# Where blocks of channel mixing stand in a unit of attention: behind its transposes, or between the second transposing step and the third score step

## The chip, the cores and the metric

The kernel runs on one core of a Trainium2 chip. The metric is the device time of one execution in microseconds. Five engines work side by side, each through its own instructions in program order: PE (TensorE, matmuls), ACT (ScalarE), DVE (VectorE), POOL (GpSimd) and SP (SyncE, which here only issues DMAs).

## What is computed

Attention with pooled queries, then a Fourier mixing over tokens and channels, then a normalised two-layer channel mixing. B = 4, H = 8, 1152 keys, 576 pooled queries, head size 64, model width 512, hidden width 2048:

```
q_pool = q.reshape(B, H, S // 2, 2, D).mean(axis=3)
attn   = softmax(q_pool @ k^T / sqrt(D))
x      = (attn @ v), heads side by side           # 4 x 576 x 512
u      = x + real(fft over tokens and channels of x)
un     = (u - mean(u)) / sqrt(var(u) + 1e-6)
out    = u + max(un @ w_ch1, 0) @ w_ch2
```

## The kernel before

**Units.** Attention goes by pairs of heads (16 pairs) and by tiles of 128 queries: a unit (pr, j) is query tile j of both heads of pair pr; j = 4 is the half tile of 64 queries, with both heads in one tile. So there are 80 units of five kinds. `attention` (L292 to 374) is a generator that walks over the units. While it handles unit i it also computes the scores of unit i + 1 (`nxt`).

**Steps of a unit.** A *score step* (`s_piece`, L183) computes 384 of the 1152 keys' scores for both heads into two PSUM banks (six matmuls, L191), and DVE reads each bank into the SBUF tile `sp` with a running minimum (L197). There are three per unit. A *transposing step* (`t_step`, L220) transposes eight 128-key chunks of one head (16 small matmuls, L225) into two banks, which ACT or DVE copies into `pt` (L228); there is one for each head, and a third, *one-chunk step* for the ninth chunk of both (4 matmuls, copied into `ptc`). Then the exponentials of the next unit are issued on ACT (`s_exp`, L209), which need all three score pieces. Last comes the *value product* (`av`, L234, 36 matmuls, L242), which reads `pt` and `ptc` and is copied out by ACT (L248). For j < 3 the order on PE is: score, transpose, score, transpose, score, one-chunk transpose, value product. Where the next unit is a j = 4 one, all three scores come first; in a j = 4 unit there is one large transposing step only.

**Banks.** Seven PSUM banks, tag "t", are handed out in rotation to score pieces, transposes, blocks and the matmuls of transform and norm (`bank`, L90). An eighth belongs to the value product.

**What runs beside attention.** When four pairs (one batch) are done, `mid` (L753) does the transform (`dft`, L391) and the normalisation (`norm`, L493) of that batch, as a list of small operations, mostly on DVE, with matmuls in between. Then `ffn` (L667) supplies the channel mixing in *blocks* of 12 matmuls (L663 to 665): one of the first product ends with a relu on ACT (L685) and a subtraction on DVE (L686), one of the second with an addition on DVE (L700). A converter splits weights into two parts on ACT, DVE and POOL (L587 to 625), and a block loads the weights of later ones through SP (L654).

**What sets the order.** All instructions are put in program order by hand: engines follow the order in which the Python code issues them. `spend(pe)` (L795) is called after each step with its planned PE time (530 for a score step, 60 for a transposed chunk, 3 x 700 or 3 x 380 for the value product); it adds `pe * RATES[nb]` to a credit, where RATES is 0.98, 0.85, 0.8, 0.8 for 1 to 4 batches begun (L59), and moves a planned clock on, by which due events and operations of `mid` are issued (`pulse`, L800). Where `attention` yields, `background` (L822) issues blocks as long as credit is above zero; a block advances the clock by `half` = 1360 and costs twice that in credit. Once `lag[0]` is 0, matmuls of `mid` wait for such a place too (L805 to 809).

**Before and after the first batch.** `lag[0]` is 1 at first: value products run one unit late, and no blocks exist. When the first batch's normalised values are `ready`, `lag[0]` becomes 0 (L373). From then on a unit yields twice: at L369, behind the one-chunk transposes and ahead of the value product, and at L374, at its end. L369 is what the change touches:

```
            if not lag[0] or len(held) > 1:
                if not lag[0] or ready:
                    yield 0
                while len(held) > (lag[0] if nxt else 0):
                    finish(*held.popleft())
```

Of the kernel before, what the change touches and what calls it, by code (L numbers as in the profile page):

```python
# [54 lines left out]
def fused_kernel(ctx: ExitStack, tc: tile.TileContext, k2, q2, v2, w1, w2, cst, out):  # L55
# [34 lines left out]
    def bank(name="f"):  # L90
        return ps_t.tile([P, 512], F32, tag="t", name=name)
# [16 lines left out]
    def load_pair(pr):  # L108
        b, h = divmod(pr, H // 2)
        kh, kl, qr, kr, vs = alloc_pair()  # L110
        ds = [nc.gpsimd.dma_start(kh, k2[b, h]), nc.sync.dma_start(qr, q2[b, h]),
              nc.sync.dma_start(kr, k2[b, h]), nc.sync.dma_start(vs, v2[b, h])]
        if pr == 1:
            for d in ds:
                later(d)
        raw[pr] = kh, kl, qr, kr, vs
# [11 lines left out]
    def load_first():  # L128

        kh, kl, qr, kr, vs = alloc_pair()  # L130
        qh, ql = alloc_q()
        qkv[0] = kh, kl, qh, ql, vs

        def q_load(a, b):
            nc.sync.dma_start(qr[:, :, a:b], q2[0, 0][:, :, a:b])

        def q_part(a, b):
            eng = nc.gpsimd if a else nc.vector
            eng.tensor_tensor(qr[:, 0, a:b], qr[:, 0, a:b], qr[:, 1, a:b], op=ALU.add)
            nc.scalar.copy(qh[:, a:b], qr[:, 0, a:b])  # L140
            eng.tensor_tensor(ql[:, a:b], qr[:, 0, a:b], qh[:, a:b].bitcast(F32), op=ALU.subtract)  # L141

        def k_load(a, b):
            nc.sync.dma_start(kr[:, a:b], k2[0, 0, :, a:b])

        def k_part(a, b):
            nc.scalar.copy(kh[:, a:b], kr[:, a:b])
            for c in (slice(a, a + 192), slice(a + 192, b)) if a else (slice(a, b),):
                (nc.gpsimd if a else nc.vector).tensor_tensor(kl[:, c], kr[:, c], kh[:, c].bitcast(F32), op=ALU.subtract)  # L149

        def v_load():
            nc.sync.dma_start(vs, v2[0, 0])

        return q_load, q_part, k_load, k_part, v_load

    def prep_pair(pr):
        kh, kl, qr, kr, vs = raw.pop(pr)
        qh, ql = alloc_q()
        HW = QW // 2
        halves = (slice(0, HW), slice(HW, QW))  # L160
        for c in halves:
            nc.gpsimd.tensor_tensor(qr[:, 0, c], qr[:, 0, c], qr[:, 1, c], op=ALU.add)
        for i in range(4):
            c = slice(i * HT, i * HT + HT)
            nc.gpsimd.tensor_tensor(kl[:, c], kr[:, c], kh[:, c].bitcast(F32), op=ALU.subtract)
        qkv[pr] = kh, kl, qh, ql, vs

        def q_high():
            nc.scalar.copy(qh, qr[:, 0, :])
            for c in halves:  # L170
                nc.gpsimd.tensor_tensor(ql[:, c], qr[:, 0, c], qh[:, c].bitcast(F32), op=ALU.subtract)
        after(2600, q_high)
# [7 lines left out]
    def unit_tiles(pr, j):  # L180
        return [(2 * pr, j), (2 * pr + 1, j)] if j < 4 else [(2 * pr, 4)]

    def s_piece(pr, j, pc):  # L183
        kh, kl, qh, ql, _ = qkv[pr]
        tiles = unit_tiles(pr, j)
        c = slice(pc * 384, pc * 384 + 384)
        rows = [slice(0, D), slice(D, P)] if j < 4 else [slice(0, P)]
        ps = [bank("s")[:, :384] for _ in rows]
        for i, (q, k) in enumerate(((qh, kh), (ql, kh), (qh, kl))):
            for p, r in zip(ps, rows):  # L190
                nc.tensor.matmul(p, lhsT=q[r, j * P:j * P + P], rhs=k[r, c], start=i == 0, stop=i == 2)  # L191
        for p, k in zip(ps, tiles):
            if pc == 0:
                sp[k] = spp.tile([P, S], F32, tag="sp", name="sp")
                bia[k] = smp.tile([P, 3], F32, tag="bia", name="bia", bufs=6)
            bt = bia[k]
            nc.vector.tensor_scalar(  # L197
                sp[k][:, c], p, -0.0625, bt[:, pc - 1:pc] if pc else None,
                op0=ALU.mult, op1=ALU.min, accum_out=bt[:, pc:pc + 1],
            )  # L200
        return 530

    def s_exp(n, j):
        pr = n // 2
        if pr not in den:
            den[pr] = smp.tile([P, 9], F32, tag="den", name="den", bufs=3)
        t = sp[n, j]
        col = 5 * (n % 2) + j
        last_exp[0] = nc.scalar.activation(t, t, AF.Exp, bias=bia.pop((n, j))[:, 2:3], scale=-1.0,  # L209
                                           accum_out=den[pr][:, col:col + 1]).ins  # L210

    lag = [1]
# [79 lines left out]
    def attention():  # L292
        idle = gp.tile([P, 512], F32, tag="g", name="zero")
        nc.vector.memset(idle, 0.0)
        ps = bank()
        for n in (512, 512, 192):
            nc.tensor.matmul(ps[:, :n], lhsT=idle[:, :P], rhs=idle[:, :n], start=True, stop=True)
        q_load, q_part, k_load, k_part, v_load = load_first()
        k_load(*K0[0])
        q_load(*Q0[0])  # L300
        for c in K0[1:]:
            k_load(*c)
        nc.sync.dma_start(ident, cst[4, :, :P])
        q_load(*Q0[1])
        v_load()
        q_load(*Q0[2])
        units = [(pr, j) for pr in range(NP) for j in range(5)]
        k_part(*K0[0])
        q_part(*Q0[0])
        k_part(*K0[1])  # L310
        k_part(*K0[2])
        for pc in range(3):
            s_piece(0, 0, pc)
        q_part(*Q0[1])
        s_exp(0, 0)
        s_exp(1, 0)
        nc.sync.dma_start(onesm, cst[4, :, P:2 * P])
        q_part(*Q0[2])
        yield 2000
        held = deque()  # L320
        for i, (pr, j) in enumerate(units):
            if pr == 1 and j == 0:
                for x, (t, r) in enumerate(((cc1, P), (cs1, P), (cc2, 97), (cs2, 97))):
                    n, m = t.shape[1:]
                    for r0, r1 in ((0, r // 32 * 32), (r // 32 * 32, r)):
                        if r0 < r1:
                            nc.sync.dma_start(t[r0:r1], cst[x, r0:r1, :n * m].rearrange("p (a b) -> p a b", a=n))
            if pr + 1 < NP:
                if j == 0:
                    load_pair(pr + 1)  # L330
                if j == 2:
                    prep_pair(pr + 1)
            nxt = units[i + 1] if i + 1 < len(units) else None

            tiles = unit_tiles(pr, j)
            where = {}
            early = lag[0] and i % 2
            scores = deque(range(3) if nxt else ())

            def score():  # L340
                if scores:
                    spend(s_piece(*nxt, scores.popleft()))

            if nxt and nxt[1] == 4:
                for _ in range(3):
                    score()
            for x, k in enumerate(tiles):
                score()
                pt = t_tile(512, early)
                spend(t_step(pt, [(k, c) for c in range(8)], "av" if j < 4 and (x or lag[0] and i % 2) else "aa"))  # L350
                for c in range(8):
                    for y in (x,) if j < 4 else (0, 1):
                        where[y, c] = pt, c * D
            score()
            pt = t_tile(P, early)
            spend(t_step(pt, [(k, 8) for k in tiles], "aa"))
            for y in range(2):
                where[y, 8] = pt, y * D if j < 4 else 0
            score()
            for k in unit_tiles(*nxt) if nxt else ():  # L360
                s_exp(*k)
            for k in tiles:
                sp.pop(k)
            held.append((pr, j, where))
            if j == 4:
                after(3000 if pr % 4 < 3 else 1500, den_recip(pr))
            if not lag[0] or len(held) > 1:
                if not lag[0] or ready:
                    yield 0  # L369
                while len(held) > (lag[0] if nxt else 0):  # L370
                    finish(*held.popleft())
                    if lag[0] and ready:
                        lag[0] = 0  # L373
            yield 0  # L374
# [390 lines left out]
    ready = []  # L765
# [4 lines left out]
    def after(wait, fn):  # L770

        heapq.heappush(events, (now + wait, next(tick), fn))
# [22 lines left out]
    def spend(pe):  # L795
        nonlocal credit
        credit = min(credit + pe * RATES[nb], 4000.0)
        pulse(pe * (1.25 if lag[0] else 1.1))
# [132 lines left out]
```

## Time and profile before

| | |
|---|---|
| median of 3 runs | 967.57 us (967.31 to 971.88) |
| the profiled execution's own time | 966.58 us |
| its span in the profile | 964.8 us |
| granted TensorE clock, mean | 0.973 |
| PE busy | 905.6 us, 94% |
| DVE busy | 565.2 us, 59% |
| ACT busy | 509.6 us, 53% |
| POOL busy | 233.9 us, 24% |

Busy time is the union of an engine's instructions. Matmuls are pipelined, so their rows overlap: the time of a step is read from the start of its first matmul to the start of the next step's. A number in brackets behind a row is the idle time of the engine ahead of it, with the instruction that ended the wait. Tile names: `s` score bank, `sp` scores and exponentials, `t` transposing bank, `pt`/`ptc` transposed tiles, `o` value product, `f` banks of blocks, transform and norm.

### The profile page before, as it was taken

The numbers are of one execution on the slowest core, as the hardware profiler recorded it, in microseconds if no ns is written. First come the engines' busy times: TensorE is split into PE (matmuls) and PEld (weight loads), VectorE is DVE, ScalarE is ACT, GpSimd is POOL, SyncE is SP. The second block draws the span as 40 slices with busy tenths as digits, with TensorE's granted clock in tenths as the row PEclk, the third lists the DMA queues.
The fourth block names the chain that finished last, engine by engine and source line by source line (L and its number), as shares of the span: only waits on it lengthen the run. The fifth ranks groups of instructions, "written<-read, shape, count | busy, mean of one in ns | idle before, by whom it ended". The sixth has DMA issues, their size and how long they took to land.

```text
span 964.8 us, 22607 instructions
## 1 busy us (share of the span) xinstructions
PE 905.6 (94%) x9030; PEld 768.2 (80%) x9030; DVE 565.2 (59%) x1501; ACT 509.6 (53%) x1068; POOL 233.9 (24%) x299
## 2 busy tenths in 40 slices
PE   7998888887999979899999999999999999999998
PEld 5877777675777767688788778788887788999998
DVE  6776879877465787964645757554446633222222
ACT  6786787596476756776645547755532121101110
POOL 4045443255346263723031103030000000000000
PEclk9998998987999989989999999999999999999999
DMA  6333664343676844656454315333255456643432
GB/s 221 111 126 128 201 222 167 104 164 112 226 267 203 309 152 170 205 187 241 146 166 155 114 35 167 126 110 100 67 167 190 137 187 204 219 131 120 122 109 66
DMA packets 54413, 153.27 MB, mean 159 GB/s; under 512 B 15187, under 2 KB 18019, under 8 KB 54309
## 3 DMA queue, kind: packets, MB, share of 16 engines
q1 hardware_dynamic: 49972, 142.20, 44.2%
q0 software_dynamic: 2160, 8.85, 2.9%
q8 instruction: 71, 1.16, 0.5%
q10 hardware_dynamic: 2176, 0.79, 0.3%
q14 instruction: 34, 0.27, 0.1%
HBM read 129.06 MB, written 22.75 MB: 157 GB/s over the span
## 4 chain that ended last, share of the span: by engine, by line
PE 67%; DVE 10%; ACT 8%; DMA 7%; issue 5%; SPq 1%; POOL 1%; DVEq 0%; ACTq 0%; POOLq 0%
PE f L663 14%; PE f L665 12%; PE f L664 12%; PE o L242 10%; PE s L191 8%; PE t L225 5%; ACT sp L209 3%; DVE sp L197 3%; PE f L475 3%; DMA r<-rd 3%; DMA rd<-rs 2%; ACT pt L228 1%; DVE xs L418 1%; PE f L466 1%; SPq L273 1%
## 5 line engine op out<-in xcount | busy, mean ns | idle before, releaser
L209 ACT ACTIVATE sp<-sp,bia 128x1152 f32<-128x1152 f32 x144 | 180.5, 1256 | 42.5 <-DVE sp L197 42.1
L197 DVE TENSOR_SCALAR_CACHE_REDUCE sp<-s,bia 128x384 f32<-128x384 f32 x288 | 165.9, 613 | 11.3 <-PE s L191 7.6
L225 PEld LDWEIGHTS t<-ident,sp 64*128 64x128 f32 x2592 | 113.3, 141 | 58.8 <-DVE sp L197 24.1
L225 PE MATMUL t<-ident,sp 64*128 64x64 f32 x2592 | 127.9, 229 | 34.1 <-DVE sp L197 16.3
L242 PE MATMUL o<-pt,vs 128*64 128x128 f32 (+1 forms) x2560 | 154.3, 273 | 5.0 <-ACT x L248 2.5
L242 PEld LDWEIGHTS o<-pt,vs 128*64 128x64 f32 x2560 | 134.3, 142 | 25.4 <-issue 14.6
L228 ACT COPY pt<-t 128x512 f32<-128x512 f32 x211 | 114.6, 588 | 68.5 <-PE t L225 67.8
L686 DVE SCALAR_TENSOR_TENSOR g<-f,g 128x512 fp32r<-128x512 f32 (+1 forms) x80 | 50.8, 638 | 164.2 <-ACT g L685 164.2
L685 ACT ACTIVATE g<-f 128x512 fp32r<-128x512 f32 (+1 forms) x80 | 44.1, 553 | 194.4 <-PE f L665 194.4
L663 PE MATMUL f<-g,w 128*128 128x512 f32 (+1 forms) x320 | 123.0, 384 | 2.1 <-DVE sp L197 1.0
L663 PE MATMUL f<-unh,w 128*128 128x512 f32 (+1 forms) x320 | 122.4, 383 | 0.7 <-DVE sp L197 0.2
L664 PE MATMUL f<-unh,w 128*128 128x512 f32 (+1 forms) x320 | 118.8, 371 | 0.0
L665 PE MATMUL f<-unl,w 128*128 128x512 f32 (+1 forms) x320 | 118.7, 371 | 0.0
L664 PE MATMUL f<-g,w 128*128 128x512 f32 (+1 forms) x320 | 118.7, 371 | 0.0
L665 PE MATMUL f<-g,w 128*128 128x512 f32 (+1 forms) x320 | 118.6, 371 | 0.0
L191 PE MATMUL s<-ksh,qh 64*128 64x384 f32 (+1 forms) x432 | 105.4, 427 | 6.7 <-ACT pt L228 3.0
L197 DVE TENSOR_SCALAR_CACHE_REDUCE sp<-s 128x384 f32<-128x384 f32 x144 | 74.9, 553 | 50.9 <-PE s L191 48.8
L191 PE MATMUL s<-ksh,ql 64*128 64x384 f32 (+1 forms) x432 | 85.8, 341 | 0.6 <-POOL ql L141 0.6
L191 PE MATMUL s<-ksl,qh 64*128 64x384 f32 (+1 forms) x432 | 85.6, 341 | 0.3 <-POOL ksl L149 0.3
L700 DVE TENSOR_TENSOR x<-f,x 128x512 f32<-128x512 f32 x48 | 33.1, 689 | 76.7 <-PE f L665 76.7
L611 POOL TENSOR_TENSOR wa<-wa,wk 128x256 int32<-128x256 int32 x64 | 48.8, 783 | 107.3 <-DVE wa L607 80.8
L663 PEld LDWEIGHTS f<-g,w 128*128 128x128 f32 x320 | 60.4, 189 | 14.1 <-DVE sp L197 3.6
(110 smaller groups left out, 1342.3 us busy)
## 6 DMA issues: line engine op xcount, KB each, us to landing
w<-w SPq DMA_DIRECT2D x128, 512.0 KB
wraw<-in_w SPq DMA_DIRECT2D x32, 512.0 KB
w<-wraw SPq DMA_DIRECT2D x32, 512.0 KB
qr<-in_q SPq DMA_DIRECT2D x15, 640.0 KB
vs<-in_v SPq DMA_DIRECT2D x16, 576.0 KB
ksh<-in_k POOLq DMA_DIRECT2D x15, 576.0 KB, 6.0
kr<-in_k SPq DMA_DIRECT2D x15, 576.0 KB
out<-x SPq DMA_DIRECT2D x12, 256.0 KB
```

The source lines that it names most:

```text
L191: nc.tensor.matmul(p, lhsT=q[r, j * P:j * P + P], rhs=k[r, c], start=i == 0, stop=i == 2)
L197: nc.vector.tensor_scalar(sp[k][:, c], p, -0.0625, bt[:, pc - 1:pc] if pc else None, op0=ALU.mult, op1=ALU.min, accum_out=bt[:, pc:pc + 1],)
L209: last_exp[0] = nc.scalar.activation(t, t, AF.Exp, bias=bia.pop((n, j))[:, 2:3], scale=-1.0, accum_out=den[pr][:, col:col + 1]).ins
L225: nc.tensor.transpose(p[:, i * D:i * D + D], sp[k][r, c * P:c * P + P], ident[r, r])
L228: (nc.vector.tensor_copy if eng == "v" else nc.scalar.copy)(pt[:, x, :o], ps[x][:, :o])
L242: nc.tensor.matmul(to.rearrange("p (x q) -> p x q", x=2) if j < 4 else to, lhsT=qkv[pr][4][:, y, c, :], rhs=rhs, start=c == 0, stop=c == N ...
L611: nc.gpsimd.tensor_tensor(ai[:, c], ai[:, c], k[:, c], op=ALU.add)
L663: nc.tensor.matmul(ps, lhsT=ah, rhs=bh, start=first, stop=False)
L664: nc.tensor.matmul(ps, lhsT=al, rhs=bh, start=False, stop=False)
L665: nc.tensor.matmul(ps, lhsT=ah, rhs=bl, start=False, stop=last)
L685: nc.scalar.activation(g[:, 0, :], ps, AF.Relu)
L686: after(1000, lambda: nc.vector.scalar_tensor_tensor(g[:, 1, :], ps, 0.0, g[:, 0, :].bitcast(F32), op0=ALU.max, op1=ALU.subtract))
```

## The change

In a unit with `lag[0]` at 0, the first of the two yields stands between the second transposing step and the third score step, no longer behind the one-chunk step; in a j = 4 unit, between its large transposing step and the second score. The yield at the old place is left for the unit in which `lag[0]` is still 1 and a batch is ready. The yield at the end of the unit stays.

```diff
@@ -351,6 +351,8 @@
                 for c in range(8):
                     for y in (x,) if j < 4 else (0, 1):
                         where[y, c] = pt, c * D
+            if not lag[0]:
+                yield 0
             score()
             pt = t_tile(P, early)
             spend(t_step(pt, [(k, 8) for k in tiles], "aa"))
@@ -365,7 +367,7 @@
             if j == 4:
                 after(3000 if pr % 4 < 3 else 1500, den_recip(pr))
             if not lag[0] or len(held) > 1:
-                if not lag[0] or ready:
+                if lag[0] and ready:
                     yield 0
                 while len(held) > (lag[0] if nxt else 0):
                     finish(*held.popleft())
```

## Rows read from the trace of the kernel before

**Rows 1.** The page, first part: engine, busy us (share of the span), instructions
```profile
PE 905.6 (94%) x9030; PEld 768.2 (80%) x9030; DVE 565.2 (59%) x1501; ACT 509.6 (53%) x1068; POOL 233.9 (24%) x299
```

**Rows 2.** Busy time by stretch: from:to, length, each engine's busy us, granted clock, DMA
```profile
235.00:720.00 485.00, 462.10 (x4983) 380.16 (x4980) 299.45 (x801) 294.90 (x617) 139.39 (x175) 0.98 0.48 163
330.00:420.00 90.00, 78.64 (x828) 63.93 (x828) 75.21 (x178) 61.48 (x123) 46.48 (x54) 0.92 0.55 191
530.00:620.00 90.00, 86.16 (x962) 70.18 (x958) 59.74 (x167) 55.60 (x118) 12.45 (x16) 0.98 0.32 104
720.00:965.00 245.00, 240.03 (x1253) 219.46 (x1251) 91.03 (x192) 40.09 (x78) 0.00 (x0) 1.00 0.47 151
```

**Rows 3.** Waits of PE, 235 to 720 us: us in total, times, longest
```profile
PE t L225 <- DVE sp L197: 10.8, 11, 2.6
...
PE o L242 <- DVE pt L228: 2.0, 4, 0.9
PE f L529 <- DVE sq L523: 1.8, 2, 0.9
PE f L663 <- DVE sp L197: 1.2, 6, 0.2
```

**Rows 4.** Timeline of PE, a quiet unit: start us, us, instruction
```profile
438.77 0.45 PE L191 MATMUL s<-ksh,qh 64*128 64x384 f32 x2
...
440.95 0.42 PE L191 MATMUL s<-ksh,qh 64*128 64x384 f32 x2
...
441.56 0.28 PE L225 MATMUL t<-ident,sp 64*128 64x64 f32 x4
441.90 0.50 PE L663 MATMUL f<-unh,w 128*128 128x512 f32 x1
...
444.84 1.97 PE L242 MATMUL o<-pt,vs 128*64 128x128 f32 x32
...
446.96 0.50 PE L663 MATMUL f<-unh,w 128*128 128x512 f32 x1
```

**Rows 5.** Timeline of PE, two units with waits, in the stretches from 330 and 530
```profile
344.73 0.65 PE L225 MATMUL t<-ident,sp 64*128 64x64 f32 x14 [2.50 <-DVE sp L197]
...
348.62 0.47 PE L225 MATMUL t<-ident,sp 64*128 64x64 f32 x3 [2.59 <-DVE sp L197]
349.02 0.79 PE L663 MATMUL f<-unh,w 128*128 128x512 f32 x1
...
354.00 1.21 PE L242 MATMUL o<-pt,vs 128*64 128x128 f32 x18
...
545.43 0.65 PE L225 MATMUL t<-ident,sp 64*128 64x64 f32 x14 [1.09 <-DVE sp L197]
...
547.30 0.33 PE L225 MATMUL t<-ident,sp 64*128 64x64 f32 x3 [0.54 <-DVE sp L197]
547.83 0.70 PE L663 MATMUL f<-g,w 128*128 128x512 f32 x1 [0.20 <-DVE sp L197]
...
552.38 0.88 PE L242 MATMUL o<-pt,vs 128*64 128x128 f32 x12
```

**Rows 6.** Timeline of PE, a unit with no block ahead of its value product
```profile
499.28 0.98 PE L242 MATMUL o<-pt,vs 128*64 128x128 f32 x14 [0.39 <-ACT ptc L228]
```

**Rows 7.** Waits of PE, 20 to 235 us, before any block exists
```profile
PE t L225 <- ACT sp L209: 10.0, 13, 1.6
```

**Rows 8.** Groups by line, 235 to 720 us: instruction, count, busy us, mean ns, idle before
```profile
L209 ACT ACTIVATE sp<-sp,bia 128x1152 f32<-128x1152 f32 x84 | 105.3, 1256 | 29.3 <-DVE sp L197 29.2
L197 DVE TENSOR_SCALAR_CACHE_REDUCE sp<-s,bia 128x384 f32<-128x384 f32 x168 | 96.8, 612 | 2.6 <-PE s L191 0.4
...
L686 DVE SCALAR_TENSOR_TENSOR g<-f,g 128x512 fp32r<-128x512 f32 x32 | 22.1, 691 | 87.6 <-ACT g L685 87.6
...
L248 ACT COPY x<-o 128x128 f32<-128x128 f32 (+1 forms) x50 | 12.4, 248 | 33.0 <-PE o L242 33.0
```

**Rows 9.** Timeline at 21 us: a score step starts, VectorE starts reading its first bank
```profile
21.66 0.44 PE L191 MATMUL s<-ksh,qh 64*128 64x384 f32 x2
...
22.59 0.56 DVE L197 TENSOR_SCALAR_CACHE_REDUCE sp<-s 128x384 f32<-128x384 f32 x1 [1.40 <-PE s L191]
```

## The prediction

> **What bounds the kernel now.** I read the page first: the PE row is busy for 94% of the span [rows 1], so nothing on another engine matters unless PE waits for it. Then the busy time by stretch. The change acts only while attention and channel mixing run together, from about 235 us (where `lag[0]` becomes 0) to about 720 us; there PE works 462.1 of 485.0 us, and after 720 it works 240.0 of 245.0 [rows 2]. So 22.9 us of idle PE is all that a better order can win directly. The same rows show where it lies: 11.4 us in the 90 us from 330 and 3.8 us in the 90 us from 530, the stretches in which the transform and norm of a batch fall among the units, and there the granted clock is 0.92 and 0.98 instead of 1.00, so some PE work ran at 1.2 and not 2.4 GHz. Third, the waits of PE in the stage [rows 3]. The largest is of transposes for VectorE's reading of score pieces: 10.8 us in 11 waits. A transpose does not use the piece that is being read; it waits for its bank, one of seven in rotation. In the timeline four of the 11 (5.2 us, up to 2.50) come before the second transposing step, which takes over a bank of the first score piece, and seven (5.6 us, up to 2.59) before the third, one-chunk step, which takes over a bank of the second piece; one of the first kind and two of the second are shown [rows 5]. A block then waits once more for the next bank: 1.2 us in 6 waits. Fourth, one quiet unit in time [rows 4]: scores and transposes from 438.77, the block from 441.90, the value product from 444.84, the next block from 446.96. A block takes 444.84 - 441.90 = 2.94 us, the value product 2.12 us, a score and a transposing step (440.95 - 438.77) / 2 = 1.09 us.
>
> **The change part by part.** No instruction is added or removed; blocks, and the matmuls of transform and norm that stop there too, move from behind the one-chunk transposes to between the second transposes and the third score. I call that place the first stop, and the end of the unit, which stays, the last stop. The code paces blocks by credit: a block is issued where credit is above zero, and costs 2 x 1360 = 2720. At RATES 0.85 a unit with j < 3 now earns (3 x 530 + 2 x 480 + 120) x 0.85 = 2270 before the first stop and 3 x 700 x 0.85 = 1785 before the last, so blocks stand there in about 0.83 and 0.66 of the units. Afterwards it earns (2 x 530 + 2 x 480) x 0.85 = 1717 and 2337: about 0.63 and 0.86. The count of blocks stays; about one block in five units goes over to the last stop. Fifty units lie in the stage (50 copies behind the value product [rows 8]), thirty of them with j < 3.
>
> Bank waits before the third transposes and before the block, 5.6 + 1.2 = 6.8 us: with a block between, 2.94 us pass in which VectorE reads the second piece, so these go where the first stop has a block. With a share of 0.65 that is **-4.4 us** (bounds 0 and -6.8). What is late next is the value product, which wants VectorE's copy of the second transposes, and then the exponential of the third piece. The waits before the second transposes, 5.2 us, stand ahead of the moved block and I leave them: **0**, between -2.6 and +2.6, since VectorE now gets 2.94 us in the middle of a unit and less at its end.
>
> Clock: the block behind the 2.59 us wait takes 354.00 - 349.02 = 4.98 us and the one behind the 1.09 and 0.54 us waits 552.38 - 547.83 = 4.55 [rows 5], against 2.94 in the quiet unit: 2.04 + 1.61 = 3.65 us lost. The second of the two waits goes and the first stays, so I take half, **-1.8 us** (0 to -3.65). The Trainium skill (TensorE: Matmul & The Clock Gate, section "HAM oscillation — how this bites in real kernels") reckons the loss as half of the time at the low level. By the granted clocks the two stretches hold 0.08 x 90 x 2 + 0.02 x 90 x 2 = 18 us of low level [rows 2], so by it an estimated 9.0 us are lost and half of that is -4.5, which would put the sum 2.7 us lower. I go by the rows, because part of that time had no matmul to slow: PE was idle.
>
> Units left without a block at the first stop: there the value product follows its transposes at once and waits for their copies. The row of such a unit shows 0.39 us [rows 6]; in all 2.0 us in 4 waits [rows 3] and this one, so 2.4 / 5 = 0.48 each. Their share among units with j < 3 goes from 0.17 to 0.37: 0.20 x 30 = 6 more units, **+2.9 us** (bounds 0, where the copies are early, and 6 x 0.9 = 5.4).
>
> Cover taken away: the third score's pieces, then both exponentials, must be done before the next unit's transposes. Now block, value product and often a second block lie between. Afterwards, without a block at the last stop, only the one-chunk step, the value product and one score do: 441.90 - 440.95 = 0.95, plus 2.12, plus 0.61 (441.56 - 440.95) = 3.68 us from the start of the third score, and 1.09 more to the second transposes, 4.77. The chain: VectorE starts reading 22.59 - 21.66 = 0.93 us after the score starts [rows 9], 0.61 for the piece, 1.26 for an exponential [rows 8]: 2.80, and 4.06 for the second. That fits by 0.7 to 0.9 us. The block's own subtraction on VectorE, 0.69 us [rows 8], now stands ahead of the pieces and leaves 0 to 0.2. So a wait appears where one more operation falls in. Units with a block first and none last: (1 - 0.86) x 30 = 4, at 0 to 0.77 us, the mean of the waits for exponentials in the stage without blocks (10.0 us in 13 [rows 7]); I take 0.25: **+1.0 us** (0 to 3.1).
>
> Queues: the weight loads that a block issues on SP go out in the same order, and the events that feed POOL are run by the same planned clock; no wait of PE in the stage names a DMA or POOL [rows 3], and the block-to-block distances stay near 5 us, so I cost this at nothing; should the cover go, the price is a late weight tile. The stage before 235 us keeps its order, as the old condition and the new one both stop there only when `ready`.
>
> Sum: -4.4 + 0 - 1.8 + 2.9 + 1.0 = **-2.3 us**. The profiled execution took 966.58 us (span 964.8 and 1.8 around it), 1.0 below the median of 967.57; I set the sum against the median: **965.3 us**. About 0.5%, 4.8 us, is what a measurement of this kernel can tell from no change, so this counts as the same.
>
> **The rivals.** *The exponential becomes the wait (slower).* If transform and norm use up the credit so that the last stop is empty in half of the 50 units and not in 0.14, the pieces of the third score have only 3.68 us of cover in 25 units. For it: in the stage without blocks, with just this cover, PE waited 13 times for 0.77 us in some 29 units [rows 7]. Against it: blocks move towards that stop. Price: 25 x 13/29 x 0.77 = 8.6 us instead of 1.0, giving 972.9. The sum turns positive from some ten such units, one in five. The Trainium skill (PSUM — Partial Sum Buffer, section "Engine vs sequencer instructions") has VectorE's queue as strictly first in, first out, which would let the block's subtraction hold the pieces back; the 2.50 us that transposes waited while VectorE worked off older operations agrees [rows 5].
>
> *The busy stretches come loose (faster).* All of the 6.8 us goes, both slowed blocks run at 2.4 GHz (-3.65), and half of the 5.2 us before the second transposes goes, since VectorE is no longer behind when the next unit starts: -6.8 - 3.65 - 2.6 + 2.9 + 1.0 = -9.2, giving 958.4. For it: the two 330 us rows alone hold 5.1 us of wait and 2.0 us of slow block in one unit. Against it: VectorE has 75.2 of 90 us of work there [rows 2], and it does not get less.
>
> *The waits only move.* VectorE sets the pace in those stretches, so what is saved before the block is waited for after it: -4.4 and -1.8 vanish, +3.9 stays, 971.5. That the change does nothing at all would need credit that is never above zero at the new place; 0.63 speaks against it.
>
> **How the numbers follow.** Forecast 0.48, the exponential 0.17, the busy stretches 0.27, waits that only move 0.08. Below 962.7 counts as faster: the busy stretches and 0.06 of the forecast's own spread, 0.33. Above 972.4 as slower: the exponential and 0.02 more, 0.19. The rest, 0.48, is the same. The range reaches just past the faster rival and to the slower one: 957.5 to 972.9.
>
> **What would show it.** Right: transposes wait for score pieces fewer than 8 times in the stage and none over 1 us stands before the one-chunk step; no block takes over 4 us behind such a wait; value products wait for copies some ten times at 0.4 to 0.5 us; waits of transposes for exponentials stay under 2 us. Wrong: several microseconds of waits for exponentials, or the clock rows of 330 to 420 no higher than 0.92, or PE's idle sum near 22.9 us with other names.

## The result and the profile after

The change made the kernel slower: 978.37 us in the median (972.85 to 982.35) against 968.55 for the kernel before, a ratio of 1.0112 with a 95% interval of 1.0089 to 1.0135. The forecast of 965.3 us was wrong in sign, and the time lies above its range.

The page of the changed kernel, engines' line and the group of the value product:

```profile
PE 908.0 (93%) x9030; PEld 769.4 (79%) x9030; DVE 564.3 (58%) x1501; ACT 508.3 (52%) x1068; POOL 230.7 (24%) x299
...
L242 PE MATMUL o<-pt,vs 128*64 128x128 f32 (+1 forms) x2560 | 160.8, 276 | 14.2 <-DVE pt L228 6.3
```

The same group on the page before:

```profile
L242 PE MATMUL o<-pt,vs 128*64 128x128 f32 (+1 forms) x2560 | 154.3, 273 | 5.0 <-ACT x L248 2.5
```

Work is the same and its counts are the same [rows 1]. The value product is what grew: before it was busy for 154.3 us with 5.0 us of idle time ahead of its matmuls, now 160.8 and 14.2. Busy time is a union, so at an equal count it grows where matmuls overlap less, and where they take longer at the lower clock (1.2 GHz). In the timeline each makes up about half of the growth: 20 value products instead of 10 stall inside their run of matmuls, and 7 instead of 5 run at the lower clock.

Busy time by stretch, columns as in [rows 2]:

```profile
235.00:720.00 485.00, 457.80 (x4926) 375.31 (x4923) 291.01 (x790) 291.02 (x612) 136.25 (x174) 0.98 0.47 159
330.00:420.00 90.00, 79.31 (x807) 64.22 (x808) 72.34 (x176) 59.39 (x121) 42.23 (x55) 0.91 0.53 186
530.00:620.00 90.00, 85.67 (x961) 70.53 (x957) 61.30 (x167) 53.19 (x115) 12.36 (x14) 1.00 0.34 109
720.00:965.00 245.00, 243.95 (x1263) 221.96 (x1262) 95.71 (x195) 42.12 (x82) 0.00 (x0) 1.00 0.50 156
```

PE idles 27.2 us in the stage, before 22.9 [rows 2]. The busy stretch from 330 us is no better: 10.7 us idle instead of 11.4, and a granted clock of 0.91 instead of 0.92. Waits of PE from 235 to 720 us, columns as in [rows 3]:

```profile
PE o L242 <- DVE pt L228: 6.3, 8, 1.8
PE o L242 <- ACT ptc L228: 3.7, 7, 1.1
PE t L225 <- DVE sp L197: 3.5, 6, 1.8
...
PE t L225 <- ACT pt L228: 2.5, 1, 2.5
PE o L242 <- ACT pt L228: 1.9, 5, 0.7
PE t L225 <- ACT sp L209: 1.3, 3, 0.8
```

The bank waits that the prediction went after did shrink, from 10.8 us to 3.5. In their place stand waits of the value product for its transposed copies: 6.3 + 3.7 + 1.9 = 11.9 us, where [rows 3, 6] have 2.0 and 0.4. In the timeline the block behind the last value product starts 6.6 us later than before (at 713.57 and not 706.94), and by then 57 blocks are done instead of 58; the missing one, 2.94 us, comes behind it. That makes up the 9.6 us by which the span grew (974.4 against 964.8).

A quiet unit without a block at the first stop, on PE and then on VectorE:

```profile
696.56 0.43 PE L242 MATMUL o<-pt,vs 128*64 128x128 f32 x2
697.39 1.82 PE L242 MATMUL o<-pt,vs 128*64 128x128 f32 x29 [0.39 <-DVE pt L228]
...
699.47 0.50 PE L665 MATMUL f<-g,w 128*128 128x512 f32 x1
```

```profile
695.47 0.62 DVE L197 TENSOR_SCALAR_CACHE_REDUCE sp<-s,bia 128x384 f32<-128x384 f32 x1
...
696.01 0.61 DVE L197 TENSOR_SCALAR_CACHE_REDUCE sp<-s,bia 128x384 f32<-128x384 f32 x1
...
696.55 0.69 DVE L228 COPY pt<-t 128x512 f32<-128x512 f32 x1
```

The value product starts, does two matmuls on the first head's copy and stops for the second's, which VectorE only begins at 696.55, behind both banks of the second score step. From its first matmul to the next block it takes 2.91 us, against 2.12 in a unit with a block ahead [rows 4]: 0.79 us, of which the row shows 0.39 as idle. Counted in program order, 24 of the 47 units from (6, 3) on, the first with lag 0 throughout, have no block at the first stop, before the change 13.

The second thing to see is one unit near 350 us, where a transform's operations and the third score meet. In the kernel before:

```profile
345.19 0.42 PE L191 MATMUL s<-ksh,qh 64*128 64x384 f32 x1
...
350.68 0.60 DVE L197 TENSOR_SCALAR_CACHE_REDUCE sp<-s,bia 128x384 f32<-128x384 f32 x1
...
351.33 1.26 ACT L209 ACTIVATE sp<-sp,bia 128x1152 f32<-128x1152 f32 x1 [1.87 <-DVE sp L197]
...
360.62 1.48 PE L225 MATMUL t<-ident,sp 64*128 64x64 f32 x36
```

The same unit in the changed kernel:

```profile
350.80 0.45 PE L191 MATMUL s<-ksh,qh 64*128 64x384 f32 x2
...
352.50 0.75 DVE L420 TENSOR_TENSOR xs<-x 128x576 f32<-128x576 f32 x1
...
355.05 0.67 DVE L688 SCALAR_TENSOR_TENSOR g<-f,g 128x512 fp32r<-128x512 f32 x1
...
356.01 0.60 DVE L197 TENSOR_SCALAR_CACHE_REDUCE sp<-s,bia 128x384 f32<-128x384 f32 x1
...
356.65 1.26 ACT L209 ACTIVATE sp<-sp,bia 128x1152 f32<-128x1152 f32 x1 [4.47 <-DVE sp L197]
...
358.67 0.90 PE L225 MATMUL t<-ident,sp 64*128 64x64 f32 x17
...
361.42 1.06 ACT L228 COPY pt<-t 128x512 f32<-128x512 f32 x2
...
362.04 0.71 PE L225 MATMUL t<-ident,sp 64*128 64x64 f32 x15 [2.48 <-ACT pt L228]
...
363.70 0.79 PE L665 MATMUL f<-unh,w 128*128 128x512 f32 x1 [0.95 <-DVE g L688]
```

The third score step starts at 350.80, but VectorE reads its first bank at 356.01, behind transform operations and the block's subtraction. VectorE was as far behind before: from 345.19 to 350.68 it took 5.49 us, now 5.21. But then the third score stood ahead of the block and of what is issued during it, and from the exponential (351.33) to the next unit's transposes (360.62) there were 9.29 us, with the block, the value product and another block between. Now 2.02 us are left (356.65 to 358.67). ScalarE idles 4.47 us ahead of the exponential, what stands behind it in ScalarE's queue comes late, and PE waits 2.48 us for copies out of that queue.

### The profile page after: what moved, and what is told of

It is laid out like the page before. It is cut to its first block, busy times and chain, and to the rows that moved or that the text cites. A ratio compares the mean times of both kernels' runs of the same rounds, so it can differ in the third digit from the quotient of the medians.

```text
span 974.4 us, 22586 instructions
## 1 busy us (share of the span) xinstructions
PE 908.0 (93%) x9030; PEld 769.4 (79%) x9030; DVE 564.3 (58%) x1501; ACT 508.3 (52%) x1068; POOL 230.7 (24%) x299
## 4 chain that ended last, share of the span: by engine, by line
PE 66%; DVE 10%; ACT 9%; DMA 6%; issue 5%; POOL 2%; SPq 1%; DVEq 0%; ACTq 0%; POOLq 0%
PE f L665 13%; PE f L667 12%; PE f L666 12%; PE o L242 10%; PE s L191 8%; PE t L225 5%; ACT sp L209 3%; DVE sp L197 3%; PE f L477 3%; DMA r<-rd 2%; DMA rd<-rs 2%; ACT pt L228 1%; DVE pt L228 1%; PE f L468 1%; DVE xs L420 1%
## 5 line engine op out<-in xcount | busy, mean ns | idle before, releaser
L242 PE MATMUL o<-pt,vs 128*64 128x128 f32 (+1 forms) x2560 | 160.8, 276 | 14.2 <-DVE pt L228 6.3
L242 PEld LDWEIGHTS o<-pt,vs 128*64 128x64 f32 x2560 | 138.7, 144 | 27.3 <-ACT ptc L228 9.1
L191 PEld LDWEIGHTS s<-ksh,qh 64*128 64x128 f32 (+1 forms) x432 | 48.8, 190 | 35.2 <-issue 18.9
```

Of the source, the lines that this page charges most:

```text
L242: nc.tensor.matmul(to.rearrange("p (x q) -> p x q", x=2) if j < 4 else to, lhsT=qkv[pr][4][:, y, c, :], rhs=rhs, start=c == 0, stop=c == N ...
```

## The experiments

Two theories. *Share*: moving the stop lets less credit build up ahead of it, so more units have no block there, and these pay with a wait in the value product. *Place*: a block ahead of the third score holds back that score and what hangs on it. "Empty" below is the number of the 47 units with no block at the first stop. Each ratio is to the kernel before, measured beside it (its median was 966.3 to 968.6 us), with its 95% interval.

| run | place of blocks | empty | median us | ratio |
|---|---|---|---|---|
| before | old | 13 | 968.55 | 1 |
| changed kernel | new | 24 | 978.37 | 1.0112 (1.0089 to 1.0135) |
| lent_credit | new | 14 | 972.93 | 1.0055 (1.0033 to 1.0078) |
| old_place_held_back | old | 26 | 979.34 | 1.0124 (1.009 to 1.0158) |
| both_stops | new, else old | 15 | 971.16 | 1.0032 (1.0014 to 1.005) |
| last_stop_only | end of unit | 47 | 999.61 | 1.0334 (1.0297 to 1.0371) |
| blocks_new_mid_old | new | 15 | 971.5 | 1.0055 (1.0037 to 1.0073) |
| mid_new_blocks_old | old | 18 | 976.94 | 1.0112 (1.0083 to 1.0141) |
| old_place_lent_650 | old | 8 | 964.91 | 0.9986 (0.9962 to 1.001) |
| old_place_lent_2000 | old | 7 | 962.52 | 0.9954 (0.9934 to 0.9975) |
| new_place_when_quiet | new / old | 14 | 968.82 | 1.0017 (0.9996 to 1.0037) |
| new_place_when_mid | old / new | 13 | 971.17 | 1.0038 (1.0019 to 1.0057) |
| mid_waits_for_third_score | new | 14 | 965.17 | 0.9985 (0.9971 to 0.9999) |
| mid_waits_lent_2000 | new | 7 | 971.13 | 1.0055 (1.0031 to 1.0078) |

### The share at either place

The new place with the old share:

```diff
             if not lag[0]:
+                lent = 650 * RATES[nb]
+                credit += lent
                 yield 0
+                credit -= lent
```

> The blocks stay at the new place, but the credit that the third score and the one-chunk step earn (650 x RATES) is lent ahead of the first stop and taken back behind it, so that blocks divide over the two stops as before the change: 14 units without a block at the first stop (from unit (6, 3) on), where the changed kernel has 24 and the kernel before 13. Theory 'share' (the loss is units left without a block at the first stop, whose value product waits for the copies of its transposes): the waits inside value products fall from some 25 us back to 10 to 13, the bank waits stay at the changed kernel's level, and the time comes to 963 to 969 us. Theory 'place' (a block ahead of the third score holds back that score's readers, the exponentials and the transform's work, whatever its share): 975 to 980 us, no better than the changed kernel.

The old place with the new share:

```diff
                 if not lag[0] or ready:
+                    held_back = 0.0 if lag[0] else 650 * RATES[nb]
+                    credit -= held_back
                     yield 0
+                    credit += held_back
```

> The kernel before, with its blocks at the old place behind the one-chunk step, but 650 x RATES of credit held back at the first stop and given back behind it, so that blocks divide as in the changed kernel: 26 units without a block at the first stop. Theory 'share': the value products of the 13 added units wait 0.6 us each in quiet stretches and 1 to 3 us in busy ones, so 974 to 981 us, as slow as the changed kernel or a little slower. Theory 'place': 966 to 970 us, no change from before.

Both stops kept, from the changed kernel:

```diff
-                if lag[0] and ready:
+                if not lag[0] or ready:
                     yield 0
```

> The changed kernel with the yield at the old place kept as well, so a unit has three stops, and a block that finds no credit at the new place may still come ahead of the value product: 15 units are left without a block at either. Theory 'share': 963 to 969 us, near the run with lent credit. Theory 'place': 973 to 980 us, since most blocks (and all transform matmuls) still stand at the new place.

No first stop (the same line of the kernel before, the other way round):

```diff
-                if not lag[0] or ready:
+                if lag[0] and ready:
                     yield 0
```

> The kernel before with no first stop at all once lag is 0: all blocks and transform matmuls stand at the end of a unit, so all 47 units from (6, 3) on are without a block ahead of the value product. Theory 'share': 34 more units than before with 0.6 us each in quiet and 1 to 3 us in busy ones, 20 to 45 us in all, less some bank waits: 985 to 1010 us. Theory 'place': nothing stands ahead of the third score, so no loss of that kind: 966 to 975 us.

Share is confirmed where blocks never left the old place: with 26 empty units it is as slow as the changed kernel, 0.0124 x 968 = 12.0 us for 13 more units, 0.92 us each; with 47 it is 32 us for 34, 0.95 each. At the new place, from lent credit to the changed kernel, ten more empty units cost 0.0057, some 5.5 us or 0.55 each; the intervals are too wide to tell this from 0.92. The waits of the last run from 235 to 720 us show where:

```profile
PE o L242 <- DVE pt L228: 15.4, 22, 3.1
PE o L242 <- ACT pt L228: 6.4, 13, 0.9
...
PE o L242 <- ACT ptc L228: 2.9, 7, 0.5
```

24.7 us of value products waiting for copies, against 2.4 before. But with the old share at the new place only about half of the loss goes: 1.0055, or 972.93 us, between the 963 to 969 of *share* and the 975 to 980 of *place*; with both stops kept, 971.16 lies there too. Both theories hold a part. The waits with lent credit:

```profile
PE t L225 <- ACT pt L228: 4.9, 3, 2.5
PE o L242 <- DVE pt L228: 4.5, 7, 1.5
PE t L225 <- ACT sp L209: 4.0, 6, 1.6
PE t L225 <- DVE sp L197: 3.4, 4, 2.0
```

The 7.4 us that bank waits lost (10.8 to 3.4) are paid back by transposes that wait for exponentials and for ScalarE's copies, 8.9 us, which are not among the waits of [rows 3].

### What the place costs

Blocks and transform matmuls put at different places, by a yield that names what may be issued (`'f'` blocks, `'m'` transform and norm). Blocks at the new place:

```diff
                 credit += lent
-                yield 0
+                yield 'f'
                 credit -= lent
...
-                if lag[0] and ready:
+                if not lag[0]:
+                    yield 'm'
+                elif ready:
                     yield 0
```

> As the run with lent credit, but the transform's and the norm's matmuls stop at the old place behind the one-chunk step and only blocks stop at the new one (15 units without a block at the first stop). It asks what is left of the loss, some 4.5 us, once the share is restored. Theory 'transform' (its matmuls and the VectorE and ScalarE work tied to them, ahead of the third score, delay that score's readers and the next exponentials in the stretches around 330 and 570 us): 965 to 969 us, the loss is gone, and waits of transposes for exponentials fall from 4.0 to under 2 us. Theory 'block work' (the relu, subtraction or addition behind a block does it): 971 to 974 us, as with lent credit.

and the reverse, from the kernel before:

```diff
+            if not lag[0]:
+                yield 'm'
             score()
...
-                if not lag[0] or ready:
+                if not lag[0]:
+                    yield 'f'
+                elif ready:
                     yield 0
```

> The complement: blocks at the old place as before, the transform's and the norm's matmuls at the new one; the credit that these use up leaves 14 units with neither a block nor such matmuls at the first stop, against 9 before. Theory 'transform': 972 to 977 us (4.5 us for the place and some 4 for the share). Theory 'block work': 969 to 973 us, only the share's part.

Neither matmul kind is the cause alone. With the transform's matmuls back at the old place, nothing was won over lent credit (1.0055 both times), against the theory that they do it; and moving them alone costs 1.1%, the upper end of what that theory gave, some of it probably through five more units that have neither block nor such matmuls ahead of the value product.

Then the new place in quiet units only (`not mids`), and in the others only (`mids` in that condition):

```diff
-            if not lag[0]:
+            here = not lag[0] and not mids
+            if here:
...
-                if lag[0] and ready:
+                if not lag[0] and not here or lag[0] and ready:
                     yield 0
```

> Blocks at the new place (with lent credit) only in units that begin their first stop with no transform or norm in progress; in all others at the old place. 14 units without a block, as before the change. Theory 'third score late in the busy stretches' (with a block ahead of it, the third score's pieces are read behind the transform's operations that are issued during the block, its exponentials come late, and the copies queued behind these on ScalarE with them): the busy stretches go as before, so 965 to 969 us, no loss. Theory 'the place costs everywhere': 970 to 973 us, as with lent credit in all units.

> The complement: the new place (with lent credit) only where a transform or norm is in progress, the old place in quiet units; 13 units without a block. Theory 'third score late in the busy stretches': 970 to 974 us, the whole loss of lent credit. Theory 'everywhere': 967 to 970 us.

The loss splits as 0.17% and 0.38% (each give or take 0.2%): the units during a transform or norm carry some two thirds, and in quiet units the loss can't be told from none. The last step takes away what stands between the third score and its reading there, with blocks still at the new place:

```diff
+            free = not lag[0] and not held_mid
             if not lag[0]:
+                held_mid.append(0)
                 lent = 650 * RATES[nb]
                 credit += lent
                 yield 'f'
                 credit -= lent
             score()
+            if free:
+                held_mid.clear()
```

> As the run with blocks at the new place and the transform's matmuls at the old one, but no operation of transform or norm is issued from the first stop until the third score has been issued, so VectorE reads its pieces behind the block's own operation alone; 14 units without a block. Theory 'third score late': the 2.5 us wait of transposes for copies near 360 us goes and the time falls from 971.5 to 966 to 969 us. If it is the block's own operation, or only the moved order of other work: 970 to 973 us.

965.17 us, a ratio of 0.9985: the whole loss of the place is made up, from 1.0055 for the same kernel without the hold. In the unit near 350 us VectorE reads the third score's first bank 2.72 us behind the step's start:

```profile
348.26 0.45 PE L191 MATMUL s<-ksh,qh 64*128 64x384 f32 x2
...
350.98 0.60 DVE L197 TENSOR_SCALAR_CACHE_REDUCE sp<-s,bia 128x384 f32<-128x384 f32 x1
```

So the operations of transform and norm that are issued between the second transposes and the third score are what the place's cost hangs on, as far as these runs go. One rival is not ruled out: the hold may win time of its own, wherever the blocks stand, and no run holds these operations with the blocks at the old place. The granted clock speaks for such a part. Over the eleven executions it is 0.980 of full speed in the mean, without the hold 0.975, in the kernel before 0.975 to 0.977; the stretch from 330 us, columns as in [rows 2], first without the hold, then with it:

```profile
330.00:420.00 90.00, 78.97 (x795) 63.21 (x791) 68.59 (x172) 56.51 (x116) 43.14 (x52) 0.92 0.52 178
```

```profile
330.00:420.00 90.00, 80.89 (x851) 65.25 (x846) 70.70 (x175) 58.77 (x122) 45.31 (x53) 0.96 0.54 189
```

By these two rows an estimated 0.04 x 90 = 3.6 us at most of the 6.3 us between the two medians come from the clock. The single wait that I had named did not go: near 360 us transposes still stand 2.5 us, now ended by a block's subtraction on VectorE. Other waits did: for ScalarE's copies 4.3 us of transposes went, and those of the transform's own matmuls fell from 3.6 to 0.4; in their stead bank waits grew from 2.1 to 5.1 and waits for exponentials from 0.9 to 4.6. The waits of PE in this run:

```profile
PE t L225 <- DVE sp L197: 5.1, 5, 1.8
PE t L225 <- ACT sp L209: 4.6, 4, 2.0
PE o L242 <- DVE pt L228: 4.0, 7, 1.1
PE t L225 <- DVE g L698: 2.5, 1, 2.5
```

### A share in the other direction, at both places

More blocks at the old place, with 650 and with 2000 lent:

```diff
                 if not lag[0] or ready:
+                    lent = 0.0 if lag[0] else 2000 * RATES[nb]
+                    credit += lent
                     yield 0
+                    credit -= lent
```

> The kernel before, blocks at the old place, with 650 x RATES of credit lent ahead of the first stop and taken back behind it: 8 units without a block there instead of 13, 40 blocks there and 18 at the last stop. If the share works in the other direction too, two or three units with j < 3 lose their wait of 0.6 to 1 us and a busy one may lose more: 964 to 967.5 us. If the exponentials were the limit (the last stop is empty more often), 969 to 973 us.

> As the run before it with 2000 x RATES lent: 53 of 58 blocks at the first stop, 7 units without one, and only 5 blocks left at the last stop. Share: as good as with 650, 963 to 967 us. Cover of the exponentials: behind the first stop only the value product and one score stand ahead of the next unit's transposes, but at the old place the third score is older by a block, so waits for exponentials stay under 2 us and the time under 968; if they do not, some 40 units at 0.3 to 0.8 us give 975 us or more.

and at the new place, with the hold of the run above:

```diff
-                lent = 650 * RATES[nb]
+                lent = 2000 * RATES[nb]
```

> The best form of the new place so far (transform and norm held until the third score is issued, their matmuls at the old place) with 2000 x RATES lent, as in the fastest run at the old place: 7 units without a block at the first stop, 47 blocks there and 11 at the last stop. Share alone: three to six microseconds below the run with 650 lent, 959 to 963 us. Cover of the exponentials: with the last stop empty in some 38 units, a block ahead of the third score leaves only 3.7 us from its start to the next unit's transposes; if that is too little, waits for exponentials rise from 4.6 us to 10 to 20 us in all, and the time is 966 to 980 us, where the same share at the old place gave 962.5 us.

With 2000 lent at the old place the kernel takes 962.52 us, a ratio of 0.9954 (0.9934 to 0.9975): faster than both kernels, with 53 of 58 blocks at the first stop. With 650 the gain is not clear of zero. The same share at the new place loses 0.55%. The waits tell the two apart; first the old place, then the new:

```profile
PE t L225 <- DVE sp L197: 10.0, 10, 2.5
...
PE o L242 <- DVE pt L228: 1.6, 3, 0.9
```

```profile
PE t L225 <- ACT sp L209: 10.3, 10, 2.8
PE t L225 <- DVE sp L197: 3.4, 3, 3.0
...
PE o L242 <- DVE pt L228: 1.1, 1, 1.1
```

At the old place no wait for exponentials is listed at all; at the new one they are 10.3 us, once the last stop is empty in most units. By these waits, a block behind the third score and ahead of the value product covers both the copies of this unit and the exponentials of the next. Ahead of the third score it covers the copies alone, and the exponentials need another block at the end of the unit.

## Why the prediction was wrong

**The step that failed** is the bank waits' -4.4 us, and the clock's -1.8 that hangs on it: waits that go were counted as time won. The run with lent credit tests the terms of the place alone, with 14 empty units against 13. For these the prediction has -4.4 + 0 - 1.8 + 1.0 = -5.2 us; the run took 0.55% more, +5.3 us. The waits went, and more than forecast: 10.8 + 1.2 us fell to 3.5 + 0.5 in the changed kernel, and to 3.4 with lent credit. But 8.9 us of waits of transposes for exponentials and copies came with lent credit, for which the sum had +1.0. That VectorE's backlog sets the pace in the busy stretches, so that PE waits for its next result instead, fits these rows but is argued from them. It is the rival *the waits only move*, which I had given 0.08, and even its 971.5 us lie below the time measured.

**Units left without a block at the first stop, +2.9.** The direction was right, the size too small; by the difference between lent credit and the changed kernel it was some 5.5 us for ten units. The count: six more units of j < 3 were forecast, and program order has seven (7 to 14); but one of j = 3 and three of j = 4 came on top, which I had left out. The price: I took 0.48 us each from five waits, the idle part only. A quiet unit loses 0.79 from start to start, and the kernel before already showed it: the value product of [rows 6] takes 2.90 us to the next block, not 2.12.

```profile
498.46 0.43 PE L242 MATMUL o<-pt,vs 128*64 128x128 f32 x2
...
501.36 0.50 PE L663 MATMUL f<-unh,w 128*128 128x512 f32 x1
```

In busy stretches it can be more. One value product near 418 us, in a unit without a block before the change too, waited 1.81 us at once, behind 0.36. Another, in a unit that lost its block, follows waits of 1.80 and 0.67 us and has no idle time itself, but runs at the lower clock (granted 0.77 from 330 to 345 us) and takes 4.83 us:

```profile
336.20 4.26 PE L242 MATMUL o<-pt,vs 128*64 128x128 f32 x31
...
341.03 0.79 PE L665 MATMUL f<-g,w 128*128 128x512 f32 x1
```

At the 0.92 each of the old place the eleven units would have been +10.1 us and the sum +4.9, at 0.55 each +6.1 and +0.9. So this term alone, sized right, does not give the 9.8 us measured.

**Clock, -1.8.** Next to nothing came. By the prediction's own reckoning the two stretches hold 18 us of low level before and 0.09 x 90 x 2 = 16.2 us after: 0.92 became 0.91 in the stretch from 330 us, and 0.98 became 1.00 in the one from 530, where idle time was 4.3 us against 3.8. The slow block near 548 us has gone; instead of the one at 349.02 the block at 363.70 is slow, behind waits of 2.48 and 0.95 us, with 5.42 us to the next transposes (369.12).

**Cover taken away, +1.0.** Under-sized, and for another reason than I gave. I let only the block's own operation stand ahead of the third score's pieces, and took the 0.93 us from score to reading out of a stage without blocks. The transform's operations stand ahead too: near 350 us it is 5.49 us before and 5.21 after, which 9.29 us of cover hid before and 2.02 do not hide now. Holding these operations back took the loss from 1.0055 to 0.9985, with the rival named there.

**The rivals.** *The exponential becomes the wait* had the right side and the wrong condition: in the changed kernel the last stop is filled in most units, and waits for exponentials are 1.3 us. Its price is real where its condition holds: 10.3 us in the run with 2000 lent. *The busy stretches come loose* did not happen. Two signs of being right came all the same: transposes waited for score pieces 6 times, and for exponentials 1.3 us. They were signs about the waits that had been looked at, and the time went to others. Two signs of being wrong came as well, the clock row at 0.91 and an idle sum of 27.2 us under other names.

**Queues.** That loads and POOL cost nothing fits the waits after: none of those shown names a DMA or POOL as what PE waited for.

## What to carry to other kernels

When a filler is issued where a credit is positive, moving the place also moves how much credit has built up there; count the units that are left without a filler, and price them by the start-to-start time of the step that loses its cover, not by its idle rows. Ask of each place which waits one filler covers at once: here the place behind the last score covered two and the earlier place one, and the gain lay in putting more fillers at the old place. Where an in-order engine is behind, as VectorE seems to be here, do not count a wait on it as won before it is clear that its next result is not waited for instead.

## What the runs showed of the hardware that was not expected

A stall inside a run of small matmuls is only partly idle time in the profile. The value product at 696.56 us took 0.79 us longer than one without a wait, and its rows show 0.39 us idle. About half of the 6.5 us by which the group's busy time grew over the kernel (154.3 to 160.8, with the same 2560 matmuls) is of this kind; the other half is value products at the lower clock.
